# Another written order for tiles 1 to 6 of an attention-plus-MLP kernel, with VectorE's weight sums in other places

## The chip, the cores and the metric

The kernel runs on one core of a Trainium2 chip. The metric is the device time of one execution in microseconds (us), taken as the median of several runs. The core's engines work side by side, each on its own queue in the order in which the program was written: TensorE (PE, matrix products), VectorE (DVE), ScalarE (ACT), GpSimd (POOL) and SyncE (SP, which here only issues DMAs). They wait for each other through semaphores.

## The reference, cut to what matters

```python
# q, k, v: 8 batches x 8 heads x 576 rows x 64
q_s = softmax(q, axis=-1)          # over the 64
k_s = softmax(k, axis=2)           # over the 576 rows
kv  = einsum('bhsd,bhse->bhde', k_s, v)
att = einsum('bhsd,bhde->bhse', q_s, kv)
x   = att.transpose(0, 2, 1, 3).reshape(4608, 512)
h   = x @ w_in                     # 512 x 2048
out = maximum(0.01 * h, h) @ w_out # 2048 x 512
```

Inputs and output are float32 in HBM; the kernel's products are bf16.

## The kernel before, in words

The attention goes batch by batch (b = 0 to 7). The two layers go in nine tiles of 512 tokens (t = 0 to 8). Batch 0, batch 1 and tile 0 are written out call by call and end at about 50.5 us of the profile. Tiles 1 to 6, with the attention of batches 2 to 7 between them, are played from one long list of words, `SCORE` (L799); tiles 7 and 8 from a second list, `WEAVE`. `play` (at the end of the kernel function) takes a word at a time and emits its instructions. A list thus fixes the order on every engine's queue at once; a scheduler does not touch it. Moving a word past words of other engines changes nothing, moving it past words of its own engine does. Rotating buffers are also given out in this order: six PSUM banks for most products (two more for others), six SBUF slots of 9216 bytes per partition for the raw loads and later for sums (`raw`), three output buffers.

The words with a tile number in front (`of_tile`, here for tile t):

- `u<h><p>`: one block of layer 1 on TensorE (`layer1`, L516), four matmuls of 512 columns into one bank (448 in tile 1). `l<h><p>`: the leaky activation that empties it, on ScalarE (`leaky`, L525).
- `P<n><sub><half>`: layer 2 on TensorE (`behind`, L946), four matmuls of 256 columns. Layer 2 is done with seven half-size products instead of eight (a Winograd scheme), so products 5, 6, 7 and 3 take differences of activations: `n0_p` to `n3_p`, subtractions on VectorE (L1003). Product 5 needs n0, product 6 needs n1.
- `q...`: ScalarE copies a partial sum out of PSUM (L1013, L1005). `d...`: VectorE adds the last partial sum and writes an output buffer (L895). `w0`, `w1`: SyncE stores it, four DMAs.
- In tile 6 layer 1 too has seven products: `m<n>_p` (TensorE, L916), `s...` (ScalarE, L980) and `c...` (VectorE, L895).

The words of the attention (`of_batch`, for batch b):

- `lk`, `lq`, `lv`: SyncE issues the load of k, q or v (1152 KB each, L83).
- `kt.0` to `kt.3`: VectorE's tree of maxima over k (L160); `km`: the rest of that maximum (L165 to L185); `ks`, `ksB`: the maximum is subtracted from k (L193), on VectorE for batches 2 to 4 and on GpSimd for 5 to 7; `ke`: exp (ScalarE, L201); `va`, `vb`: v is cast (ScalarE, L211); `kv`: TensorE's k-by-v product (L294); `kr`, `kd`: its normalisation (VectorE L326, ScalarE L332).
- `qm`: row maxima of q (VectorE, L225); `qs`: their subtraction, on GpSimd (L256); `qe`: exp (ScalarE, L264); `qu`: row sums and reciprocals (VectorE, L273, L275); `qn`: normalisation (VectorE, L280, two inputs in SBUF); `qt`: a transposing DMA, issued by SyncE (L457); `A`: TensorE's product that makes the tile's input (L438); `x`: ScalarE copies it out (L429). Batch 2 has q in two parts, `.0` and `.1`.
- `T3` (L666), `F1` to `F4` (`fsums`, L780) and `X6`, `X7`: VectorE's sums over weights and inputs for the seven-product schemes. An `F` subtracts two 128x2048 blocks of w_in in bf16, both in SBUF. Tile 6 is the first user of the F sums.

GpSimd's queue in this part holds ten subtractions: qs2.1, qs2.0, qs3, qs4, ks5, qs5, ks6, qs6, ks7, qs7.

Of the kernel before, what the change touches and what calls it, by code (L numbers as in the profile page):

```python
# [25 lines left out]
def kernel(  # L26
# [772 lines left out]
    SCORE = """  # L799
        1u00 1l00 1u11 1u10 1l10 1l11 1u02 1u04 1u15 kt2.1 kt2.2 kt2.3 1u05 qm2.1 1u12 1l02 qs2.1 qm2.0 1u07  # L800
        1l04 1l15 km2 1u06 qe2.1 1l05 1u13 1l12 qu2.1 qs2.0 qe2.0 1u03 ks2 lk3 1l13 1u01 1l06 1l07 1l01 1u17
        1l17 1l03 1u14 1l14 1u16 1l16 ksB2 1P100 qu2.0 qn2.0 1P101 1P110 1P111 1P200 ke2 1P201 1P210 1n0_0
        1n0_1 qn2.1 1P500 1P501 1P510 1n1_0 lq3 1n1_1 1P211 va2 qt2.0 1q1 1P511 1P600 vb2 1q5 1n3_0 kv2
        1P601 qt2.1 1P300 1n2_0 kr2 1P610 1P611 1n3_1 1P301 1d11 kd2 A2.0 A2.1 A2.2 1P310 1q6 x2.01 x2.00
        1P311 x2.20 T3 lq4 1P700 1n2_1 x2.21 1P701 lv3 1P710 1P711 x2.11 kt3.0 kt3.1 kt3.2 kt3.3 qm3 x2.10
        2u02 2l02 2u12 2l12 2u03 2l03 2u06 2u00 qs3 1d22 1P400 1P401 1P410 va3 vb3 2l00 2l06 qm4 qe3 km3
        1d12 2u14 lk4 1w0 1P411 qs4 2u04 2l04 2u13 2l14 2u01 2l01 2u11 2u07 2l13 qu3 lv4 2u15 2u05 2l11 1q21
        2l05 2l15 2u17 2l17 2l07 ks3 2u10 2l10 2u16 2P100 qn3 2P101 qt3 lk5 2l16 ksB3 ke3 2P200 2n0_0 2n0_1
        2P201 2P210 2P211 2n1_0 2P110 2P111 2q1 2n2_1 2n1_1 2P500 2P501 2d11 2P510 kv3 kr3 2P600 2n3_0 2P511
        2n2_0 kd3 2P601 kt4.0 kt4.1 2P610 2q5 2P611 lk6 A3.0 A3.1 2n3_1 A3.2 2q6 2P300 x3.20 x3.10 x3.01  # L810
        kt4.2 2P700 2P701 2P710 x3.21 1w1 2P711 2P301 2P310 lq5 2P311 x3.11 kt4.3 x3.00 3u02 3l02 2d22 km4
        2P400 ks4 va4 2P401 2P410 2P411 3u00 qe4 ksB4 kt5.0 kt5.1 kt5.2 2q21 lv5 kt5.3 km5 ks5 vb4 3l00 3u06
        3u03 3l03 3u07 qu4 3l06 3u17 3l17 3u01 3l01 2d12 3u11 3l07 3l11 3u10 ke4 3l10 3u04 3l04 3u12 3l12
        3u05 3u14 3l05 kv4 kr4 kd4 3l14 3P100 3u13 3l13 3u15 3u16 3l16 qn4 lq6 3P101 3P110 lv6 3l15 3P200
        2w0 qt4 3P111 3P201 3n0_0 3n0_1 3P210 3P211 3n1_1 3n1_0 3P500 3P501 3P510 3P511 3q1 3P600 3n3_1
        3n3_0 2w1 3P601 kt6.0 va5 vb5 3P610 3q5 ke5 3P611 3d11 3P300 3P301 3P310 A4.0 A4.1 3q6 A4.2 kv5
        3n2_0 3n2_1 x4.00 x4.01 3P311 x4.20 x4.11 kt6.1 3P700 3P701 3P710 3P711 x4.21 x4.10 4u03 lq7 va6
        kt6.2 kt6.3 qm5 4u13 4u02 3d22 qs5 3P400 3P401 3P410 vb6 3P411 4l02 4l13 kr5 kd5 3d12 4l03 4u12 4l12
        4u10 4u00 qe5 4u06 4l06 4l00 4l10 4u16 4u17 4u05 4u01 km6 lk7 qu5 qn5 ks6 4l16 3q21 4u04 4l17 4l04
        4l05 4u07 kt7.0 4l07 4u11 4u15 4l01 4l11 4n0_0 4u14 4l15 4l14 4n0_1 4P100 4P101 4P110 4P500 4P111  # L820
        4q1 4n2_0 4n1_0 lv7 4n1_1 4n2_1 kt7.1 4n3_1 kt7.2 ke6 4P501 4P510 4n3_0 4P511 4P600 kt7.3 4P601
        4P610 4P611 4q6 qt5 A5.0 A5.1 A5.2 4q5 x5.10 kv6 qm6 x5.11 x5.01 3w0 qs6 4P700 4P701 4P710 4P711
        x5.00 x5.21 4P300 4P301 4P310 4d22 km7 x5.20 4P200 4P201 4P210 va7 vb7 kr6 kd6 4P400 4P401 4P211
        4P410 4P411 5u00 5l00 5u02 5l02 5u01 5l01 qe6 4d11 5u06 ks7 4P311 F1 qm7 5u12 qs7 5u07 5l06 5l07
        4q21 qu6 4w1 4d12 5l12 5u03 5l03 5u10 ke7 5u05 5u04 5l04 5u16 qn6 3w1 5l10 5l16 5l05 5u13 5l13 5u15
        5u11 5l11 5u17 5l17 5n0_0 5u14 5n2_0 5l15 5P100 5P101 5P110 5P111 5n2_1 5l14 5n0_1 5P500 5P501 5q1
        5P510 5n1_0 5P600 5n1_1 5P601 5P610 5n3_1 5P611 5q6 qt6 A6.0 x6.00 A6.1 x6.10 A6.2 F2 x6.01 kv7
        x6.20 5P200 x6.21 5P511 x6.11 5P700 5q5 qe7 5P701 5P201 5P210 5P710 5P211 5P711 F3 F4 5n3_0 X6.0 Z0
        X6.1 X6.2 X6.3 kr7 6m5_0 6s5_0 6m5_1 Z1 5d22 6m1_0 5P300 5P301 5P400 6s5_1 kd7 5P401 6m1_2 6m1_1
        6s1_1 5P410 5d11 5P411 6s1_0 5P310 qu7 qn7 qt7 5P311 6m1_3 6s1_2 6m6_2 6m6_0 5q21 Z2 6s6_2 6m2_0 4w0  # L830
        6s6_0 6s1_3 5d12 6c11_0 6l11_0 6m3_0 6c12_0 6m2_1 6m6_1 6c11_1 6m6_3 6s6_1 6m3_1 6m5_3 6c12_1 6s6_3
        6m2_3 6c11_3 6l11_1 6m7_1 6c22_1 6l12_0 6s5_3 6m5_2 6s5_2 6m2_2 6c11_2 6l11_3 6l12_1 6m7_2 6l11_2
        6c22_2 6l22_1 6m3_3 6c12_3 6m3_2 6l12_3 6m7_0 6c22_0 6l22_0 6l22_2 6m7_3 6P100 6c22_3 6P101 5w0
        6m4_1 6m4_0 6l22_3 6P110 6P111 6c12_2 6l12_2 6m4_2 6n0_0 6n1_0 6q1 6l21_1 6m4_3 6l21_0 6P500 6n0_1
        6n1_1 6P600 6P501 6P510 6l21_3 6P601 6P610 6l21_2 6n2_0 6P611 A7.0 A7.1 6q6 A7.2 6P511 x7.20 6P700
        6n2_1 x7.21 6P701 x7.00 6n3_0 6P710 6P711 6q5 6d22 6P200 6P201 5w1 6P210 6P400 x7.11 x7.01 x7.10
        X7.0 X7.1 X7.2 6P401 6P410 6P411 X7.3 6P211 6n3_1 6P300 6q21 6w1 6P301 6P310 6P311 6d11 6d12 6w0
    """.split()
# [304 lines left out]
```

## Time and profile before

| | us |
|---|---|
| median of 3 runs (268.37 to 268.96) | 268.94 |
| the profiled execution | 269.27 |
| its span in the trace | 267.5 |
| busy: TensorE, VectorE, ScalarE, GpSimd | 256.0, 224.7, 192.8, 63.0 |
| granted TensorE clock, mean | 0.995 |

The span is what the trace covers; the remaining 1.77 us of the execution lie around it. "Busy" is the time in which an engine had an instruction running. An engine that waits for a semaphore is idle, but one whose instruction has started and cannot go on counts as busy. The views used are the page, the list of waits, the sums by window, the timeline and the trace's events for DMA landings. A row of the timeline gives start, duration, engine, line of the kernel, operation, output<-inputs, sizes and how many instructions are merged; in brackets stands the idle time just before it and what ended it.

### The profile page before, as it was taken

Reading aid. Unit: us, or ns where it says so; the run is one execution under the profiler, and the core shown is the slowest. Engines: PE = TensorE matmul, PEld = TensorE weight load, DVE = VectorE, ACT = ScalarE, POOL = GpSimd, SP = SyncE. Lnnn points to the kernel's source line nnn. Section 1 sums busy time; section 2 is a strip of 40 time slices with the busy share of each in tenths; the row PEclk is TensorE's granted clock in tenths of the full one; section 3 lists DMA queues with packets and bytes.
Section 4 is the critical chain, followed back from the end, with each engine's and each line's share of the span. In section 5 each row is a group of like instructions: output and inputs, shape, how many; then the busy total and the mean of one; then the engine's idle time right before and its main releaser. Section 6 shows DMA issues by size and latency. Waiting matters only on the chain.

```text
span 267.5 us, 6287 instructions
## 1 busy us (share of the span) xinstructions
PE 256.0 (96%) x2559; PEld 188.9 (71%) x2570; DVE 224.7 (84%) x358; ACT 192.8 (72%) x367; POOL 63.0 (24%) x45
## 2 busy tenths in 40 slices
PE   8689999999999999999999999989999999999992
PEld 3167754457864687458888884478888888888882
DVE  2997899799998998989938989998996589779952
ACT  3977893799769766978797669939697379628920
POOL 2485442250038000250490075600000000000000
PEclk9999999999999999999999999999999999999998
DMA  6999999998983899899952500640194050042004
GB/s 228 349 211 356 316 211 270 340 312 277 258 317 75 234 296 347 283 328 172 340 200 47 122 0 2 157 88 6 22 206 98 22 137 0 2 97 63 0 2 158
DMA packets 37645, 46.48 MB, mean 174 GB/s; under 512 B 18160, under 2 KB 21232, under 8 KB 37616
## 3 DMA queue, kind: packets, MB, share of 16 engines
q1 hardware_dynamic: 32976, 36.64, 47.7%
q0 software_dynamic: 4320, 8.91, 13.3%
q10 hardware_dynamic: 320, 0.52, 0.6%
q8 instruction: 20, 0.33, 0.5%
q14 instruction: 9, 0.07, 0.1%
HBM read 36.70 MB, written 9.44 MB: 172 GB/s over the span
## 4 chain that ended last, share of the span: by engine, by line
PE 78%; DVE 8%; DMA 6%; ACT 2%; issue 1%; POOL 0%; ACTq 0%; POOLq 0%
PE acc L946 36%; PE ph L516 24%; PE ph L916 14%; DMA w_in_sb<-in_moe_w_in_dram 3%; DMA qX<-qe 3%; DVE fs_spare L780 2%; PE po L438 2%; DVE qe L280 1%; DVE qsum L273 1%; DVE qmax L225 1%; DVE gs L1003 1%; PE pkv L294 1%; ACT ke L201 1%; PE po L294 1%; DVE k_raw L380 1%; PE pout L541 1%
## 5 line engine op out<-in xcount | busy, mean ns | idle before, releaser
L516 PE MATMUL ph<-xT,w_in_sb 128*128 128x256 bf16 (+3 forms) x505 | 85.6, 325 | 0.9 <-DMA w_in_sb<-in_moe_w_in_dram 0.2
L516 PEld LDWEIGHTS <-w_in_sb 128*128 128x128 bf16 x512 | 49.8, 98 | 32.8 <-DMA w_in_sb<-in_moe_w_in_dram 0.7
L525 ACT ACTIVATE gj<-ph 128x512 bf16<-128x512 f32 (+2 forms) x116 | 60.4, 580 | 16.3 <-PE ph L516 11.7
L946 PEld LDWEIGHTS <-gs 128*128 128x128 bf16 x512 | 49.4, 98 | 7.7 <-DVE gs L1003 1.1
L256 POOL TENSOR_TENSOR q_raw<-q_raw,qmax 128x2304 f32<-128x2304 f32 (+3 forms) x10 | 29.7, 2975 | 65.5 <-DVE qmax L225 65.5
L946 PEld LDWEIGHTS <-gj 128*128 128x128 bf16 x384 | 37.4, 98 | 5.9
L946 PE MATMUL acc<-w_out_sb,gj 128*128 128x256 bf16 x256 | 32.0, 273 | 0.0
L946 PE MATMUL acc<-wsum,gs 128*128 128x256 bf16 x256 | 30.9, 273 | 0.8 <-DVE gs L1003 0.8
L946 PE MATMUL acc<-w_out_sb,gs 128*128 128x256 bf16 x256 | 31.1, 273 | 0.0
L980 ACT COPY part_spare<-ph 128x512 f32<-128x512 f32 x36 | 19.5, 588 | 12.3 <-PE ph L916 12.0
L895 DVE TENSOR_TENSOR part_spare<-ph,part_spare 128x512 f32<-128x512 f32 x36 | 23.6, 685 | 2.6 <-PE ph L916 1.8
L273 DVE TENSOR_REDUCE qsum<-qe 128x36 f32<-128x2304 bf16 (+4 forms) x11 | 19.7, 1791 | 4.9 <-ACT qe L264 4.7
L895 DVE TENSOR_TENSOR out_sb<-acc,keep 128x512 f32<-128x512 f32 (+1 forms) x26 | 16.5, 639 | 8.5 <-PE acc L946 4.2
L1003 DVE TENSOR_TENSOR gs<-gj 128x1024 bf16<-128x1024 bf16 (+1 forms) x40 | 22.1, 577 | 1.3 <-ACT gj L525 1.3
L280 DVE TENSOR_TENSOR qe<-qe,qrec 128x2304 bf16<-128x2304 bf16 (+4 forms) x12 | 22.4, 1864 | 0.3
L1003 DVE TENSOR_TENSOR gs<-gj,gs 128x1024 bf16<-128x1024 bf16 (+1 forms) x40 | 22.2, 577 | 0.3
L1013 ACT COPY keep<-acc 128x512 f32<-128x512 f32 x22 | 12.8, 589 | 12.5 <-PE acc L946 11.9
L429 ACT CAST xT<-po 128x512 bf16<-128x512 f32 (+3 forms) x47 | 18.6, 494 | 4.2 <-PE po L438 4.0
L193 POOL TENSOR_TENSOR k_raw<-k_raw,kall 128x2304 f32<-128x2304 f32 x3 | 15.2, 5070 | 26.3 <-ACT gj L525 26.3
L916 PEld LDWEIGHTS <-fs_spare 128*128 128x128 bf16 x192 | 18.8, 98 | 2.2
L225 DVE TENSOR_REDUCE qmax<-q_raw 128x36 f32<-128x2304 f32 (+4 forms) x11 | 19.6, 1792 | 0.4 <-DMA q_raw<-in_q_dram 0.4
L916 PE MATMUL ph<-xs_spare,fs_spare 128*128 128x256 bf16 x144 | 19.2, 273 | 0.0
(89 smaller groups left out, 319.3 us busy)
## 6 DMA issues: line engine op xcount, KB each, us to landing
out_dram<-out_sb SPq DMA_DIRECT2D x68, 128.0 KB, 2.4
q_raw<-in_q_dram SPq DMA_DIRECT2D x6, 1152.0 KB, 7.0
v_raw<-in_v_dram SPq DMA_DIRECT2D x6, 1152.0 KB, 6.2
k_raw<-in_k_dram SPq DMA_DIRECT2D x5, 1152.0 KB, 9.0
w_in_sb<-in_moe_w_in_dram POOLq DMA_DIRECT2D x4, 512.0 KB, 7.9
...
```

The lines of the kernel that those rows point to most:

```text
L225: nc.vector.tensor_reduce(out=m, in_=st[b]["q"][:, :, rs], axis=AX.X, op=ALU.max)
L256: eng.tensor_tensor(out=qs, in0=qs, in1=st[b]["qmax", rs.start].unsqueeze(3).to_broadcast([P, HL, n, D]), op=ALU.subtract,)
L273: nc.vector.reduce_sum(out=qsum, in_=st[b]["qe"][:, rs], axis=AX.X)
L280: eng.tensor_tensor(out=qes, in0=qes, in1=st[b]["qrec", rs.start].unsqueeze(3).to_broadcast([P, n, HL, D]), op=ALU.mult,)
L429: eng.copy(out=o, in_=i)
L516: nc.tensor.matmul(ph[:, n0:n1], lhsT=w_in_sb[:, i, j * P : (j + 1) * P], rhs=xT[:, i, (c0 + n0) % NX : (c0 + n0) % NX + n1 - n0], start=( ...
L525: nc.scalar.activation(out=o, in_=ph, func=AF.Prelu, alpha=LEAKY_SLOPE)
L895: nc.vector.tensor_tensor(out=o, in0=x, in1=y, op=ALU.add)
L916: nc.tensor.matmul(bank[x, t, p][:, jj], lhsT=lhs(k, 2 * p + jj), rhs=rhs[:, k], start=(first and k == 0 and jj == 0), stop=(k == 1), skip ...
L946: nc.tensor.matmul(b[:, at_], lhsT=lhs(k)[:, sub * P : (sub + 1) * P], rhs=rhs[:, k], start=(first and k == 0 and at_ == 0), stop=(k % (NK ...
L980: nc.scalar.copy(out=fill(t, kind, p), in_=bank["Z" if kind == "s5" else "X", t, p])
L1003: nc.vector.tensor_tensor(out=o, in0=x, in1=y, op=ALU.subtract)
```

## The change

Only the list `SCORE` is changed: the same words in another order. No instruction is added or removed, and no function is changed. On TensorE and the other engines every instruction up to the start of tile 1 and all of `WEAVE` keep their places. GpSimd's ten subtractions keep their order among themselves. What moves, engine by engine, as far as the prediction speaks of it:

| | before | after |
|---|---|---|
| VectorE around F1 | 4d22 km7 kr6 4d11 **F1** qm7 qu6 4d12 qn6 5n0_0 5n2_0 5n2_1 5n0_1 5n1_0 ... | 4d22 kr6 km7 qm7 4d11 4d12 qu6 qn6 5n0_0 5n1_0 5n3_0 5n2_0 5n0_1 5n1_1 **F1** 5n3_1 5n2_1 F2 F3 F4 |
| VectorE in tile 2 | qu3 ks3 qn3 ksB3 2n0_0 2n0_1 2n1_0 ... | qu3 ks3 ksB3 2n0_0 qn3 2n0_1 2n1_0 2n1_1 ... |
| TensorE, layer 2 of tile 5 | 5P100 to 5P111, then 5P500 5P501 ... | 5P500, then 5P100 to 5P111, 5P501 ... |
| SyncE's loads and stores | lk3 lq3 qt2.0 qt2.1 lq4 lv3 lk4 1w0 lv4 qt3 lk5 lk6 1w1 lq5 lv5 lq6 lv6 2w0 qt4 2w1 lq7 lk7 lv7 qt5 3w0 ... | lq4 lk3 qt2.0 qt2.1 lq3 lv3 lk4 lv5 lq5 lv4 1w0 qt3 lk5 lk6 1w1 qt4 lv6 2w0 2w1 lq6 lq7 lk7 3w1 qt5 lv7 3w0 ... |

The diff, cut to the rows with the places above:

```diff
     SCORE = """
-        1u00 1l00 1u11 1u10 1l10 1l11 1u02 1u04 1u15 kt2.1 kt2.2 kt2.3 1u05 qm2.1 1u12 1l02 qs2.1 qm2.0 1u07
-        1l04 1l15 km2 1u06 qe2.1 1l05 1u13 1l12 qu2.1 qs2.0 qe2.0 1u03 ks2 lk3 1l13 1u01 1l06 1l07 1l01 1u17
...
-        1P311 x2.20 T3 lq4 1P700 1n2_1 x2.21 1P701 lv3 1P710 1P711 x2.11 kt3.0 kt3.1 kt3.2 kt3.3 qm3 x2.10
-        2u02 2l02 2u12 2l12 2u03 2l03 2u06 2u00 qs3 1d22 1P400 1P401 1P410 va3 vb3 2l00 2l06 qm4 qe3 km3
-        1d12 2u14 lk4 1w0 1P411 qs4 2u04 2l04 2u13 2l14 2u01 2l01 2u11 2u07 2l13 qu3 lv4 2u15 2u05 2l11 1q21
-        2l05 2l15 2u17 2l17 2l07 ks3 2u10 2l10 2u16 2P100 qn3 2P101 qt3 lk5 2l16 ksB3 ke3 2P200 2n0_0 2n0_1
...
-        4P610 4P611 4q6 qt5 A5.0 A5.1 A5.2 4q5 x5.10 kv6 qm6 x5.11 x5.01 3w0 qs6 4P700 4P701 4P710 4P711
-        x5.00 x5.21 4P300 4P301 4P310 4d22 km7 x5.20 4P200 4P201 4P210 va7 vb7 kr6 kd6 4P400 4P401 4P211
-        4P410 4P411 5u00 5l00 5u02 5l02 5u01 5l01 qe6 4d11 5u06 ks7 4P311 F1 qm7 5u12 qs7 5u07 5l06 5l07
-        4q21 qu6 4w1 4d12 5l12 5u03 5l03 5u10 ke7 5u05 5u04 5l04 5u16 qn6 3w1 5l10 5l16 5l05 5u13 5l13 5u15
-        5u11 5l11 5u17 5l17 5n0_0 5u14 5n2_0 5l15 5P100 5P101 5P110 5P111 5n2_1 5l14 5n0_1 5P500 5P501 5q1
...
+        1u00 1l00 1u11 1u10 1l10 kt2.1 kt2.2 1u04 1u15 1l04 lq4 1l15 kt2.3 qm2.1 1l11 qs2.1 1u05 qm2.0 1u02
+        1l05 qe2.1 1l02 1u01 1u06 1l01 km2 1u16 qu2.1 1l06 va2 1u07 1l07 qs2.0 1u03 1u14 1u12 qe2.0 1l16
+        1u13 1l12 1u17 1l03 1P100 1P101 1l13 lk3 1P110 ks2 ksB2 qu2.0 1l17 1l14 qn2.0 1n0_0 ke2 1n0_1 1P200
...
+        lv3 kt3.1 x2.01 x2.11 x2.21 1P310 1P311 kt3.2 1P700 1P701 x2.20 1P710 1P711 x2.00 x2.10 2u01 2u00
+        2l00 2u10 2l01 2l10 kt3.3 qm3 qs3 2u02 2u11 va3 2u03 1d22 lk4 2l11 1P400 1P401 1P410 1P411 2u13 2u17
+        vb3 2u12 2l02 lv5 2u06 qe3 2l03 2u16 2l06 qm4 2u04 km3 1d12 2l13 2u07 2l17 2u05 qu3 2l12 2P200 2u14
+        ks3 ksB3 lq5 2l16 2l04 2u15 1q21 2l07 2P100 2l05 2l14 2P101 2P110 2n0_0 qn3 2l15 2n0_1 ke3 2n1_0
+        2n1_1 2n2_1 2n2_0 2P201 2P111 2q1 2P500 2P210 2P211 lv4 kv3 va4 2d11 kr3 2P600 1w0 2P601 2P610 kt4.0
...
+        qt5 A5.0 4n2_1 x5.00 lv7 A5.1 A5.2 kv6 qm6 qs6 4P700 4P701 4P710 4P711 4P300 4P301 4P200 4P201 3w0
+        x5.20 4d22 4P400 4P401 4P410 4P411 x5.21 kr6 km7 kd6 ks7 x5.01 qm7 4P210 4P211 4d11 x5.11 qs7 4P310
+        x5.10 5u06 5l06 5u02 5l02 5u04 5u11 5l04 5u00 qe6 5l00 4P311 va7 4d12 qu6 5u15 5l11 5u05 qn6 5u12
+        4q21 qt6 5l15 5l12 5l05 5u10 5u13 5l13 5u03 5l03 5l10 5u01 5l01 5n0_0 5n1_0 vb7 5u16 5l16 5n3_0 5u07
+        5l07 5u14 5l14 5u17 5l17 5P500 4w1 5n2_0 5P100 5P101 5P110 5n0_1 5n1_1 F1 5P111 5P501 5P510 5P511
+        5n3_1 5q1 5P600 5P601 5P610 5P611 ke7 5q6 A6.0 x6.00 5q5 A6.1 x6.11 A6.2 kv7 x6.20 5n2_1 5P200 x6.21
...
     """.split()
```

More of the change, by code (lines that the diff above doesn't have):

```diff
@@ L799 @@
     SCORE = """
-        1u00 1l00 1u11 1u10 1l10 1l11 1u02 1u04 1u15 kt2.1 kt2.2 kt2.3 1u05 qm2.1 1u12 1l02 qs2.1 qm2.0 1u07
-        1l04 1l15 km2 1u06 qe2.1 1l05 1u13 1l12 qu2.1 qs2.0 qe2.0 1u03 ks2 lk3 1l13 1u01 1l06 1l07 1l01 1u17
-        1l17 1l03 1u14 1l14 1u16 1l16 ksB2 1P100 qu2.0 qn2.0 1P101 1P110 1P111 1P200 ke2 1P201 1P210 1n0_0
-        1n0_1 qn2.1 1P500 1P501 1P510 1n1_0 lq3 1n1_1 1P211 va2 qt2.0 1q1 1P511 1P600 vb2 1q5 1n3_0 kv2
-        1P601 qt2.1 1P300 1n2_0 kr2 1P610 1P611 1n3_1 1P301 1d11 kd2 A2.0 A2.1 A2.2 1P310 1q6 x2.01 x2.00
@@ L805 @@
-        1P311 x2.20 T3 lq4 1P700 1n2_1 x2.21 1P701 lv3 1P710 1P711 x2.11 kt3.0 kt3.1 kt3.2 kt3.3 qm3 x2.10
-        2u02 2l02 2u12 2l12 2u03 2l03 2u06 2u00 qs3 1d22 1P400 1P401 1P410 va3 vb3 2l00 2l06 qm4 qe3 km3
-        1d12 2u14 lk4 1w0 1P411 qs4 2u04 2l04 2u13 2l14 2u01 2l01 2u11 2u07 2l13 qu3 lv4 2u15 2u05 2l11 1q21
-        2l05 2l15 2u17 2l17 2l07 ks3 2u10 2l10 2u16 2P100 qn3 2P101 qt3 lk5 2l16 ksB3 ke3 2P200 2n0_0 2n0_1
-        2P201 2P210 2P211 2n1_0 2P110 2P111 2q1 2n2_1 2n1_1 2P500 2P501 2d11 2P510 kv3 kr3 2P600 2n3_0 2P511
@@ L810 @@
[L810 to L819, printed above, removed]
@@ L820 @@
-        4l05 4u07 kt7.0 4l07 4u11 4u15 4l01 4l11 4n0_0 4u14 4l15 4l14 4n0_1 4P100 4P101 4P110 4P500 4P111
-        4q1 4n2_0 4n1_0 lv7 4n1_1 4n2_1 kt7.1 4n3_1 kt7.2 ke6 4P501 4P510 4n3_0 4P511 4P600 kt7.3 4P601
-        4P610 4P611 4q6 qt5 A5.0 A5.1 A5.2 4q5 x5.10 kv6 qm6 x5.11 x5.01 3w0 qs6 4P700 4P701 4P710 4P711
-        x5.00 x5.21 4P300 4P301 4P310 4d22 km7 x5.20 4P200 4P201 4P210 va7 vb7 kr6 kd6 4P400 4P401 4P211
-        4P410 4P411 5u00 5l00 5u02 5l02 5u01 5l01 qe6 4d11 5u06 ks7 4P311 F1 qm7 5u12 qs7 5u07 5l06 5l07
@@ L825 @@
-        4q21 qu6 4w1 4d12 5l12 5u03 5l03 5u10 ke7 5u05 5u04 5l04 5u16 qn6 3w1 5l10 5l16 5l05 5u13 5l13 5u15
-        5u11 5l11 5u17 5l17 5n0_0 5u14 5n2_0 5l15 5P100 5P101 5P110 5P111 5n2_1 5l14 5n0_1 5P500 5P501 5q1
-        5P510 5n1_0 5P600 5n1_1 5P601 5P610 5n3_1 5P611 5q6 qt6 A6.0 x6.00 A6.1 x6.10 A6.2 F2 x6.01 kv7
-        x6.20 5P200 x6.21 5P511 x6.11 5P700 5q5 qe7 5P701 5P201 5P210 5P710 5P211 5P711 F3 F4 5n3_0 X6.0 Z0
-        X6.1 X6.2 X6.3 kr7 6m5_0 6s5_0 6m5_1 Z1 5d22 6m1_0 5P300 5P301 5P400 6s5_1 kd7 5P401 6m1_2 6m1_1
@@ L830 @@
[L830 to L834, printed above, removed]
@@ L835 @@
-        6n1_1 6P600 6P501 6P510 6l21_3 6P601 6P610 6l21_2 6n2_0 6P611 A7.0 A7.1 6q6 A7.2 6P511 x7.20 6P700
-        6n2_1 x7.21 6P701 x7.00 6n3_0 6P710 6P711 6q5 6d22 6P200 6P201 5w1 6P210 6P400 x7.11 x7.01 x7.10
-        X7.0 X7.1 X7.2 6P401 6P410 6P411 X7.3 6P211 6n3_1 6P300 6q21 6w1 6P301 6P310 6P311 6d11 6d12 6w0
+        1u00 1l00 1u11 1u10 1l10 kt2.1 kt2.2 1u04 1u15 1l04 lq4 1l15 kt2.3 qm2.1 1l11 qs2.1 1u05 qm2.0 1u02
+        1l05 qe2.1 1l02 1u01 1u06 1l01 km2 1u16 qu2.1 1l06 va2 1u07 1l07 qs2.0 1u03 1u14 1u12 qe2.0 1l16
@@ new lines @@
+        1u13 1l12 1u17 1l03 1P100 1P101 1l13 lk3 1P110 ks2 ksB2 qu2.0 1l17 1l14 qn2.0 1n0_0 ke2 1n0_1 1P200
+        1P201 qt2.0 1P210 1P211 1P111 1q1 qn2.1 1n1_0 1P500 1P501 1P510 1P511 1n1_1 1n3_0 1d11 1P600 vb2 kv2
+        1P601 kr2 qt2.1 1q5 lq3 1P300 1P610 1P611 1n3_1 1P301 kd2 1q6 1n2_0 A2.0 A2.1 A2.2 T3 1n2_1 kt3.0
+        lv3 kt3.1 x2.01 x2.11 x2.21 1P310 1P311 kt3.2 1P700 1P701 x2.20 1P710 1P711 x2.00 x2.10 2u01 2u00
+        2l00 2u10 2l01 2l10 kt3.3 qm3 qs3 2u02 2u11 va3 2u03 1d22 lk4 2l11 1P400 1P401 1P410 1P411 2u13 2u17
@@ new lines @@
+        vb3 2u12 2l02 lv5 2u06 qe3 2l03 2u16 2l06 qm4 2u04 km3 1d12 2l13 2u07 2l17 2u05 qu3 2l12 2P200 2u14
+        ks3 ksB3 lq5 2l16 2l04 2u15 1q21 2l07 2P100 2l05 2l14 2P101 2P110 2n0_0 qn3 2l15 2n0_1 ke3 2n1_0
+        2n1_1 2n2_1 2n2_0 2P201 2P111 2q1 2P500 2P210 2P211 lv4 kv3 va4 2d11 kr3 2P600 1w0 2P601 2P610 kt4.0
+        2P611 2q6 2P501 2P510 2P511 kd3 2q5 2n3_0 2P700 2P701 2P710 2P711 kt4.1 qt3 A3.0 x3.01 A3.1 x3.10
+        x3.00 2n3_1 kt4.2 2d22 kt4.3 km4 ks4 A3.2 ksB4 x3.21 qs4 2P300 2P301 2P310 2P311 2P400 2P401 x3.20
@@ new lines @@
+        lk5 x3.11 vb4 2P410 2P411 3u07 3u06 3l06 kt5.0 kt5.1 2q21 3l07 3u00 3l00 3u01 kt5.2 kt5.3 3l01 3u02
+        km5 2d12 3l02 3u16 3l16 3u13 3l13 qe4 3u03 3l03 3u05 lk6 3u11 3l11 3u04 3l04 1w1 3l05 3u12 3u17 3l12
+        ke4 3u10 3l17 3l10 ks5 qu4 3P100 qn4 qt4 3P101 3P110 3P111 3u14 3l14 3n0_0 3u15 3l15 3n0_1 kv4 kr4
+        3n1_0 3q1 3P200 3P201 3P210 3P500 3P501 3P211 3P510 3P511 va5 vb5 3P600 3n1_1 3P601 kd4 3q5 lv6
+        3n3_0 ke5 3n2_0 3P610 3P300 3n3_1 3P611 3P301 3d11 3q6 3P310 kt6.0 A4.0 3n2_1 x4.00 A4.1 2w0 A4.2
@@ new lines @@
+        kt6.1 kt6.2 kt6.3 kv5 3P311 x4.10 x4.20 3P700 3P701 3P710 3P711 x4.11 x4.21 x4.01 4u12 4u02 4u00 qm5
+        4u03 kr5 3d22 kd5 3P400 3P401 2w1 qs5 va6 km6 3P410 3P411 4l02 4l12 4l00 qe5 4u04 3d12 4u16 4u10
+        4l03 4l10 qu5 lq6 4u06 4u17 4l04 qn5 4u15 lq7 4l06 4l16 4l17 lk7 4u01 3q21 ks6 4l01 4n2_0 4u13 4u11
+        4l13 4l15 4u05 4l11 4n0_0 3w1 4l05 4u07 4l07 4u14 kt7.0 4l14 4P100 4P101 4P110 4P111 vb6 4n0_1 4P500
+        4n1_0 4P501 4P510 4q1 4n1_1 ke6 4P511 4q5 4P600 kt7.1 4P601 4P610 4n3_0 4P611 4q6 kt7.2 kt7.3 4n3_1
@@ new lines @@
+        5n3_1 5q1 5P600 5P601 5P610 5P611 ke7 5q6 A6.0 x6.00 5q5 A6.1 x6.11 A6.2 kv7 x6.20 5n2_1 5P200 x6.21
+        x6.10 F2 5P201 5P210 F3 x6.01 F4 qe7 5P211 5d11 5P700 5P300 4w0 kr7 X6.0 Z0 Z1 5P301 5P701 5P710
+        5P711 5P310 X6.1 5P311 X6.2 X6.3 kd7 6m5_0 6s5_0 5d22 6m5_1 6s5_1 5d12 6m1_0 6s1_0 qu7 6m1_3 6m1_1
+        6s1_1 6m2_0 5P400 6c11_0 6m6_0 6s6_0 6s1_3 6m1_2 6s1_2 6m3_0 6l11_0 6c12_0 5P401 5P410 5P411 qn7 Z2
+        6m6_2 5q21 6m5_2 6m6_1 6m2_1 6c11_1 6m3_1 6m2_3 6s6_2 6m6_3 6s6_1 6c12_1 6s5_2 6m3_2 6c11_3 6l12_0
@@ new lines @@
+        6l11_1 6m7_0 6s6_3 6m5_3 6m2_2 6l12_1 6s5_3 6c12_2 6c22_0 6l11_3 6P100 6l22_0 6c11_2 6l11_2 6m7_2
+        6m7_1 6c22_2 6l22_2 6c22_1 6l22_1 6m7_3 6c22_3 6m3_3 6c12_3 6m4_0 6m4_2 6P101 6P110 6P111 6l12_2
+        6m4_3 6n0_0 6P500 6l22_3 6n1_0 6m4_1 6l12_3 6q1 6l21_0 6n0_1 6P600 6P501 6l21_1 6P510 6n1_1 6P601
+        6P610 6P611 qt7 6l21_2 6n3_0 6l21_3 6q6 A7.0 x7.00 6n2_1 A7.1 x7.11 x7.10 6n2_0 A7.2 6P511 6q5 6P700
+        6P701 6P710 6P711 6d22 6P300 x7.01 6P200 6P201 5w0 6P400 6P401 6P410 6P411 x7.20 x7.21 X7.0 6P210
@@ L838 @@
+        5w1 X7.1 6P211 6n3_1 6P301 6q21 6w1 6P310 6P311 6d11 6d12 6w0 X7.2 X7.3
     """.split()
```

## The prediction, as it was put on record

> **What bounds the kernel now.** I read the page's busy row and clock row first, then the sums by window, the list of waits, and last the timelines round the one gap they leave.
>
> ```profile
> PE 256.0 (96%) x2559; PEld 188.9 (71%) x2570; DVE 224.7 (84%) x358; ACT 192.8 (72%) x367; POOL 63.0 (24%) x45
> PEclk9999999999999999999999999999999999999998
> ```
>
> TensorE is busy for 96% of the span at the full granted clock. Where is the rest? The sums by window give the stretch, its length, then the busy time of PE, PEld, DVE, ACT and POOL. The first window begins with the first word of the changed list, the last ends with the last product.
>
> ```profile
> 50.50:160.00 109.50, 109.19 (x1186) 79.37 (x1191) 97.86 (x153) 87.44 (x149) 31.11 (x9) 1.00 0.75 231
> 160.00:180.00 20.00, 19.10 (x117) 10.76 (x121) 19.93 (x15) 13.75 (x21) 8.42 (x2) 1.00 0.39 83
> 180.00:262.60 82.60, 82.59 (x844) 73.39 (x835) 66.08 (x119) 56.23 (x110) 0.00 (x0) 1.00 0.24 55
> ```
>
> In these 212.1 us TensorE idles 0.31 + 0.90 + 0.01 = 1.22 us. The 0.31 are gaps of 0.05 us that the chain of waits puts down to "issue"; at those places matmul records are missing (the next start comes two spacings later), so they are no idle time. A second reading, by the starts: a `u` word takes 0.865 us, a `P` or `m` word 0.437, and nearly every word follows the one before at just that distance. One does not: from 5P500 to 5P501 it is 1.45 us instead of 0.437, **1.01 us** too many. The list of waits names it (total, times, longest), and TensorE's timeline shows it:
>
> ```profile
> PE acc L946 <- DVE gs L1003: 0.8, 1, 0.8
> ```
>
> ```profile
> 175.48 0.60 PE L946 MATMUL acc<-wsum,gs 128*128 128x256 bf16 x4
> 176.93 0.83 PE L946 MATMUL acc<-wsum,gs 128*128 128x256 bf16 x6 [0.85 <-DVE gs L1003]
> ```
>
> So whatever the new order does to VectorE, it can win about 1.0 us and no more, as long as TensorE's words keep their lengths. Why was VectorE late? Its timeline and GpSimd's:
>
> ```profile
> 159.42 6.04 DVE L780 TENSOR_TENSOR fs_spare<-w_in_sb 128x2048 bf16<-128x2048 bf16 x1
> 165.38 2.54 DVE L225 TENSOR_REDUCE qmax<-q_raw 128x36 f32<-128x2304 f32 x1
> 167.84 2.54 DVE L273 TENSOR_REDUCE qsum<-qe 128x36 f32<-128x2304 bf16 x1
> 171.25 3.21 DVE L280 TENSOR_TENSOR qe<-qe,qrec 128x2304 bf16<-128x2304 bf16 x1
> 174.38 2.48 DVE L1003 TENSOR_TENSOR gs<-gj 128x1024 bf16<-128x1024 bf16 x4
> 178.71 1.22 DVE L780 TENSOR_TENSOR fs_spare<-w_in_sb,fs_spare 128x2048 bf16<-128x2048 bf16 x1
> ```
>
> ```profile
> 159.31 5.07 POOL L193 TENSOR_TENSOR k_raw<-k_raw,kall 128x2304 f32<-128x2304 f32 x1
> 168.00 4.05 POOL L256 TENSOR_TENSOR q_raw<-q_raw,qmax 128x2304 f32<-128x2304 f32 x1 [3.62 <-DVE qmax L225]
> ```
>
> The last VectorE row is F2, 1.22 us; F1, of the same size, took 6.04. F1 started 0.11 us after GpSimd's ks7 and ended 1.08 us after it: for 4.82 us it stood still. qn6 (3.21 instead of the 2.54 of qn3) started 0.80 us before the end of qs7, and qn4 (3.10) 0.69 us before the end of ks5. Each has two inputs in SBUF. VectorE instructions with one input (qm, qu, 2.54 us) or with an input in PSUM (`d` words, 0.63 to 0.69) ran beside GpSimd at their usual length. After F1 the queue qm7, qu6, 4d12, qn6, then the subtractions of tile 5, runs without a gap over 0.1 us up to 5n0_1 (176.19 to 176.87), for which 5P501 waits.
>
> **The change, part by part.** I add the rows up in the new order: TensorE's words at the distances above (`kv` 0.76, `A` 0.2 to 0.3) from 50.53 us on; a ScalarE or VectorE word starts when the one before it allows (start to start is its duration less 0.12 on ScalarE and 0.08 on VectorE, as back-to-back rows overlap), or 0.20 us after the end of the TensorE word that it waits for (the distance in released rows). The same sum for the old order gives margins like the trace's (5P200 behind x6.00: 0.00, trace 0.05; 2P700 behind 2q6: 0.27, trace 0.32). It leaves out 0.09 us at each change of product kind, so its times fall behind the trace's by 0.7 us up to 175; margins do not feel that.
>
> *F1.* In the new VectorE order it stands behind 5n0_1. That one needs 5l17, which ends at 173.85 in this sum. GpSimd's last subtraction, qs7, ends at 172.05 in the old trace and earlier now, since qm7 no longer stands behind F1. F1 therefore costs 1.22: VectorE wins 4.82 us ahead of tile 5's subtractions, none of it in itself end time.
>
> *5P501.* TensorE reaches it at 175.24 (5P500, now first, at 173.05; four `P` words and the rest of 5P500 between). 5l17 173.85, then 5n0_1 0.1 + 0.69: 174.65. Margin 0.6, so the 1.01 us go.
>
> *What is late next.* Every hand-over of the new order, in the same way: 5P200 behind x6.00 0.0 (as before), 6P700 behind 6q6 0.27 (as before), kv2 behind vb2 0.35 (before 0.40), 3P201 behind 3l15 0.42, 6P300 behind 6q5 0.46, 4P501 behind 4n0_1 0.6, kv3 behind ke3 0.70. None is negative. I take zero for all; the ends are zero and what the rivals price.
>
> *GpSimd collisions left.* ks5 ends at 115.1, qn4 starts at 115.5; ks6 ends at 139.9 and qn5 starts there; qs7 ends at 167.6 and qn6 starts 0.4 us before. The last lengthens qn6 to about 3.0; 5n0_0 behind it waits for 5l01 (170.5) anyway. Zero; without that cover 0.4 of VectorE's time, against a margin of 1.7 at 5P500.
>
> *SyncE's queue.* lq3 is moved behind lk3, qt2.0 and qt2.1, to the place that lq4 had: issue 67.8, and lq4's data landed 5.9 us later, 73.7. qm3 wants it at 75.1. Cover 1.4 us; before, lq3 landed 9.7 us ahead of use. lv5 and lq5 come forward, into a stretch where they wait for vb2 (68.0) and vb3 (80.7); lv4 waits for qe3 (84.0) and is wanted by va4 at 95.0. 3w1 (2.5 us on SyncE, free at 141.2) now stands ahead of qt5; qt5 is issued at 143.8 and lands 4.6 us later (its row before: 144.4 to 149.0), A5.0 comes at 151.0. lk6 holds up 1w1 and qt4 until vb4 (103.4), long before qn4 (118) releases qt4. All zero.
>
> *VectorE in tile 2.* qn3 goes ahead of 2n0_1 to 2n1_1, ksB3 ahead of qn3. With qm3 at 75.1, qs3 ends at 81.8, qe3 at 84.0, qu3 at 87.0, ksB3 at 89.5, qn3 at 92.5, 2n1_0 at 93.8; 2P600 wants it at 94.8. Margin 1.0; zero.
>
> *X7.2 and X7.3* go behind 6d12 into the idle 0.69 us ahead of 7c11_0, which waits for 7s1_0 there. They fill 0.76. Zero to 0.1.
>
> **Sum.** 269.27 - 1.01 = 268.26 us for the profiled execution, span 266.5. That execution lies 0.33 above the median of the runs shown, so the median comes to **267.9**. About 0.3% (0.8 us) is what a measurement of this kernel can tell from no change; the forecast lies just beyond it.
>
> **Rivals.**
>
> *A new wait eats the gain.* TensorE now arrives 1.0 us earlier at everything behind 5P501. The hand-overs with margins under 0.5 are the candidates, each against a sum good to some 0.1 us; two or three small waits of 0.1 to 0.5 would leave 268.2 to 268.9. Against it: the old order had as many margins of this size, and its trace shows no wait at them. 0.17.
>
> *Slower: lq3 lands late.* The whole path qm3, qs3, qe3, qu3, qn3, 2n1_0 hangs on it, with 1.0 us to spare; beyond that each us costs TensorE one. Loads with nothing ahead of them on the queue landed in 5.3 to 6.6 us, those behind others in 8.1 to 11.9 (lk4, third in its row). lv3, lk4 and now lv5 follow lq3 at once and could draw on the same engines. At lk4's 11.9 it lands at 79.7, 4.6 late: 3.6 us of stall, 271.5. It is slower than before by 0.3% from a landing at 77.9 on. Against it: lq4 had lv3 and lk4 behind it too. 0.16.
>
> *TensorE had room all along.* If its busy rows hid slack, a better order could win more: the weight loads of these windows fill 163.5 of 212.1 us, and even a tenth of the other 48.6 would give 263.1. Against it stand the starts, one column every 0.427 ns with nothing between. 0.02. The Trainium skill's page "Perfetto Trace Analysis", section "Identifying the Most-Contended Engine", speaks for this one: matmul busy time is a bad measure of the distance to the roofline, and the share of weight loads is to be taken (here 71%). In this trace the distance between starts decides, and it leaves no such room.
>
> *It doesn't do what it says.* F1 could meet a subtraction again: excluded above by 5l17 and qs7, unless GpSimd falls some 7 us behind (F1 starts at 175.2, qs7 ends at 167.6). 0.03, at 268.9.
>
> **Chances.** Forecast 0.62 at 267.9, its own range 267.5 to 268.3 (the three runs spread by 0.6). With the room rival, faster by over 0.3% is 0.64; within 0.3% 0.17 + 0.03 = 0.20; slower 0.16. The range runs from 267.4 to 269.2: it takes in the eaten gain and leaves out the late load and the room.
>
> **What the new profile would show.** Right: an F1 row of 1.22 us; no TensorE wait on L1003; window idle sums near 0.3; qm3 at about 75 us, A6.0 1.0 us earlier than 179.7. Wrong: a TensorE wait over 0.2 us anywhere from 50.5 us on; qm3 waiting for the load of q; 5P200 late behind x6.00; a VectorE row lengthened beside GpSimd with a TensorE wait behind it.

## The result, and the profile after

| | before | after |
|---|---|---|
| median of 5 runs, us | 268.94 (268.37 to 269.09) | 267.56 (267.43 to 267.78) |
| the profiled execution, us | 269.27 | 267.72 |
| its span, us | 267.5 | 265.7 |
| ratio of the times, 95% interval | | 0.9954 (0.994 to 0.9969) |

The kernel became 0.46% faster, between 0.31% and 0.6%. Two later measurements of the same kernel, on two other occasions, gave 0.9964 (0.995 to 0.9978) and 0.996 (0.9948 to 0.9972). The gain is thus 0.9 to 1.4 us by the medians; the prediction said 1.0.

The busy row of the page after and, further down the same page, the chain that ended last, followed back from the last instruction:

```profile
PE 256.8 (97%) x2570; PEld 189.1 (71%) x2570; DVE 219.7 (83%) x358; ACT 193.0 (73%) x367; POOL 63.0 (24%) x45
...
PE 85%; DMA 6%; ACT 2%; DVE 1%; issue 0%; POOL 0%; ACTq 0%; POOLq 0%
```

The chain's row on the page before was:

```profile
PE 78%; DVE 8%; DMA 6%; ACT 2%; issue 1%; POOL 0%; ACTq 0%; POOLq 0%
```

VectorE is busy 5.0 us less although it runs the same 358 instructions, and its share of the chain falls from 8% to 1%: the chain no longer leaves TensorE to pass through 5n0_1 and what stood ahead of it. The sums by window, with the same columns as before:

```profile
50.50:160.00 109.50, 109.50 (x1193) 79.34 (x1191) 98.69 (x152) 85.39 (x147) 31.81 (x9) 1.00 0.76 235
160.00:180.00 20.00, 20.00 (x202) 11.85 (x199) 15.21 (x17) 16.61 (x25) 7.69 (x2) 1.00 0.39 83
180.00:262.60 82.60, 81.30 (x765) 72.25 (x752) 65.20 (x119) 55.44 (x109) 0.00 (x0) 1.00 0.23 53
```

The middle window, which held 0.90 us of idle TensorE time, holds none. In the last one TensorE is idle for 1.30 us only because it is done that much sooner. The 0.31 us of "idle" time in the first window of before are gone too, and so are the missing matmul records: this trace holds all 2570. The list of waits of TensorE begins so, and no line of it names L1003:

```profile
PE pout L343 <- POOL zero L105: 1.3, 1, 1.3
PE pkv L294 <- ACT vb L211: 0.8, 1, 0.8
PE kT L354 <- DVE kmax L160: 0.7, 1, 0.7
```

All its entries lie ahead of 50.5 us, in the part that was not changed; for the time from there on the list is empty. VectorE's timeline round F1, GpSimd's, and TensorE's:

```profile
167.76 2.56 DVE L280 TENSOR_TENSOR qe<-qe,qrec 128x2304 bf16<-128x2304 bf16 x1
...
174.29 0.69 DVE L1003 TENSOR_TENSOR gs<-gj 128x1024 bf16<-128x1024 bf16 x1 [0.59 <-ACT gj L525]
175.02 0.69 DVE L1003 TENSOR_TENSOR gs<-gj,gs 128x1024 bf16<-128x1024 bf16 x1
175.63 1.22 DVE L780 TENSOR_TENSOR fs_spare<-w_in_sb 128x2048 bf16<-128x2048 bf16 x1
```

```profile
158.62 5.07 POOL L193 TENSOR_TENSOR k_raw<-k_raw,kall 128x2304 f32<-128x2304 f32 x1
163.64 4.05 POOL L256 TENSOR_TENSOR q_raw<-q_raw,qmax 128x2304 f32<-128x2304 f32 x1
```

```profile
173.46 0.60 PE L946 MATMUL acc<-wsum,gs 128*128 128x256 bf16 x4
173.90 1.91 PE L946 MATMUL acc<-w_out_sb,gj 128*128 128x256 bf16 x16
175.65 2.56 PE L946 MATMUL acc<-wsum,gs 128*128 128x256 bf16 x22
```

F1 takes 1.22 us. 5n0_1 (174.29) no longer waits behind VectorE's own backlog but for ScalarE's 5l17, and ends at 174.98; TensorE reaches 5P501 about 0.6 us later, and the three rows join without a wait. qn6 starts 0.07 us after qs7's recorded end (163.64 + 4.05) and takes its bare 2.56 us.

To compare kernels without the chance of what lies outside, I use **TensorE's stretch**: from the start of 1u00 to the start of the last product. It is 211.79 us before and 210.66 after. The profiled executions differ by 1.55 us, 1.13 of them in the stretch; the rest lies ahead of 50.5 us (0.16) and behind the last product, where nothing was changed. There the time between VectorE's last instruction and the span's end took 3.9 to 4.5 us over the first six profiles; the control run below comes back to it. Of the 1.13 us, 1.01 are the gap at 5P501, and the other 0.11 lie in the six `kv` words, which together take 4.55 us up to the next word's start before and 4.44 after.

### The profile page after: what moved, and what is told of

It is laid out like the page before. It is cut to its first block, busy times and chain, and to the rows that moved or that the text cites. A ratio compares the mean times of both kernels' runs of the same rounds, so it can differ in the third digit from the quotient of the medians.

```text
span 265.7 us, 6286 instructions
## 1 busy us (share of the span) xinstructions
PE 256.8 (97%) x2570; PEld 189.1 (71%) x2570; DVE 219.7 (83%) x358; ACT 193.0 (73%) x367; POOL 63.0 (24%) x45
## 4 chain that ended last, share of the span: by engine, by line
PE 85%; DMA 6%; ACT 2%; DVE 1%; issue 0%; POOL 0%; ACTq 0%; POOLq 0%
PE acc L946 37%; PE ph L516 29%; PE ph L916 14%; DMA w_in_sb<-in_moe_w_in_dram 3%; DMA qX<-qe 3%; PE po L438 2%; PE pkv L294 1%; ACT ke L201 1%; DVE k_raw L380 1%; PE pout L541 1%; PE po L294 1%; ACT vb L211 1%; ACT qe L264 0%; POOL w_in_sb L129 0%; DVE out_sb L895 0%
## 5 line engine op out<-in xcount | busy, mean ns | idle before, releaser
L525 ACT ACTIVATE gj<-ph 128x512 bf16<-128x512 f32 (+2 forms) x116 | 61.1, 578 | 17.8 <-PE ph L516 14.7
L1003 DVE TENSOR_TENSOR gs<-gj 128x1024 bf16<-128x1024 bf16 (+1 forms) x40 | 22.6, 579 | 4.4 <-ACT gj L525 4.4
L1003 DVE TENSOR_TENSOR gs<-gj,gs 128x1024 bf16<-128x1024 bf16 (+1 forms) x40 | 22.3, 579 | 0.5 <-ACT gj L525 0.2
L280 DVE TENSOR_TENSOR qe<-qe,qrec 128x2304 bf16<-128x2304 bf16 (+4 forms) x12 | 21.4, 1784 | 0.3
```

The lines of the kernel that those rows point to most:

```text
L280: eng.tensor_tensor(out=qes, in0=qes, in1=st[b]["qrec", rs.start].unsqueeze(3).to_broadcast([P, n, HL, D]), op=ALU.mult,)
L525: nc.scalar.activation(out=o, in_=ph, func=AF.Prelu, alpha=LEAKY_SLOPE)
L1003: nc.vector.tensor_tensor(out=o, in0=x, in1=y, op=ALU.subtract)
```

## Experiments

"Ratio" is to the kernel before, timed on the same chip in the same session. Theory: F1's stand behind ks7 is the whole loss, and its removal the whole gain. Rivals: the other moves bring something of their own; any collision of a two-input VectorE instruction with GpSimd costs its length, wherever it stands.

**F1 alone.** The kernel before, with one word moved:

```diff
-        4P410 4P411 5u00 5l00 5u02 5l02 5u01 5l01 qe6 4d11 5u06 ks7 4P311 F1 qm7 5u12 qs7 5u07 5l06 5l07
+        4P410 4P411 5u00 5l00 5u02 5l02 5u01 5l01 qe6 4d11 5u06 ks7 4P311 qm7 5u12 qs7 5u07 5l06 5l07
...
-        5P510 5n1_0 5P600 5n1_1 5P601 5P610 5n3_1 5P611 5q6 qt6 A6.0 x6.00 A6.1 x6.10 A6.2 F2 x6.01 kv7
+        5P510 5n1_0 5P600 5n1_1 F1 5P601 5P610 5n3_1 5P611 5q6 qt6 A6.0 x6.00 A6.1 x6.10 A6.2 F2 x6.01 kv7
```

> The order before, with F1 alone moved behind 5n1_1 (its place in the new order). Theory (TensorE's one wait came from F1 standing still behind GpSimd, and the time follows TensorE's waits alone): F1 takes 1.22 us, TensorE has no wait on L1003 near 175 us, 267.5 to 267.9 us, ratio 0.995 to 0.997, as the whole new order. Rival (the new order wins by its other moves, such as 5P500 first or the loads): the ratio stays over 0.998.

Measured: 267.81 us, ratio 0.9951 (0.9939 to 0.9964); TensorE's stretch 210.74. VectorE's row and TensorE's:

```profile
176.41 1.22 DVE L780 TENSOR_TENSOR fs_spare<-w_in_sb 128x2048 bf16<-128x2048 bf16 x1
```

```profile
173.65 1.91 PE L946 MATMUL acc<-w_out_sb,gj 128*128 128x256 bf16 x16
175.40 2.78 PE L946 MATMUL acc<-wsum,gs 128*128 128x256 bf16 x24
```

One word gives what all the moves gave. The same two kernels beside each other on one chip:

> The kernel before with F1 alone moved behind 5n1_1, now on one chip with the kernel after. If F1's move is the whole gain, both give the same ratio to the kernel before within 0.15%, near 0.9955 (TensorE's stretch from 1u00 to its last product about 210.7 us in both). If the other moves are worth something by themselves, the kernel after is faster by 0.3% or more.

> The kernel after, beside the run with F1 alone on one chip: ratio 0.994 to 0.997. The load lq3 landed 6.4 and 8.1 us after its issue in two profiles of this kernel; if that spread is the rule, a third profile lies between 6 and 9 us, and from about 8 us on TensorE loses what goes beyond (0.1 us so far).

Measured: 268.18 us, 0.9962 (0.995 to 0.9974), with F1 alone, and 268.00 us, 0.996 (0.9948 to 0.9972), for the kernel after; stretches 210.73 and 210.66. What the other moves bring by themselves is below what can be measured here. (In the kernel after, lq3 landed 6.0 us after its issue, at the lower edge of the 6 to 9 expected.)

**The unchanged kernel, put through the same treatment.**

> The kernel before, unchanged, as a measure of the noise and of the time behind the last VectorE instruction, which is 4.4 us in the profile before and 3.9 us in the profile after. If that 0.5 us is chance, this run shows values between 3.9 and 4.5, and the ratio lies within 0.999 to 1.001. If it belongs to the new order, it stays at 4.4.

Measured: 269.21 us, ratio 0.9999 (0.999 to 1.0008), stretch 211.75. The gap is there again in TensorE's timeline:

```profile
175.44 0.60 PE L946 MATMUL acc<-wsum,gs 128*128 128x256 bf16 x4
176.89 1.38 PE L946 MATMUL acc<-wsum,gs 128*128 128x256 bf16 x11 [0.85 <-DVE gs L1003]
```

The other question of the expectation came out against chance: the time behind VectorE's last instruction was 4.47 us, as in the kernel before (4.43), while the three profiles of the kernel after have 3.89, 4.03 and 3.97. It thus seems to go with the order. Part of the difference comes back outside the span, where both profiles of the kernel before have 1.78 us and those of the kernel after 2.06 to 2.09. Why is open.

**No ks7.** The kernel before without GpSimd's subtraction of the maximum from k of batch 7:

```diff
-        ... 5u06 ks7 4P311 F1 qm7 ...
+        ... 5u06 4P311 F1 qm7 ...
```

> The order before without ks7: the subtraction of the maximum from k of batch 7 is left out. F1 stays where it was. Theory (GpSimd's subtraction holds F1 up): F1 takes 1.22 us, no TensorE wait near 175 us, ratio 0.995 to 0.997. Rival (F1 is slow at this place for another reason, such as its operands or TensorE's reads of w_in): F1 stays near 6 us and the time at 268.9.

Measured: 268.05 us, ratio 0.9961 (0.9949 to 0.9974), stretch 210.64, no wait on L1003. F1 in its old place:

```profile
159.49 1.22 DVE L780 TENSOR_TENSOR fs_spare<-w_in_sb 128x2048 bf16<-128x2048 bf16 x1
```

So it was not the place as such, but GpSimd's instruction beside it, that made 6.04 of 1.22.

**F1 put back.** The kernel after, with F1 behind 4d11, as in the kernel before (where qm7 follows F1; here it stands ahead of 4d11):

```diff
-        ... 4P210 4P211 4d11 x5.11 qs7 ...
+        ... 4P210 4P211 4d11 F1 x5.11 qs7 ...
...
-        ... 5n0_1 5n1_1 F1 5P111 ...
+        ... 5n0_1 5n1_1 5P111 ...
```

> The new order, with F1 put back behind 4d11, where ks7 runs and qs7 follows at once. Theory: F1 stands still but TensorE does not notice, because 5n0_1 is tied to 5l17 and not to VectorE's queue. If F1 gets its turn between ks7 and qs7 it takes some 4 us (ends near 165) and the ratio stays at 0.995 to 0.996. If GpSimd goes on with qs7 first, F1 takes some 8 us (ends near 169), qn6 ends after 175, TensorE waits 2 to 3 us at 5P500 and the time is 269.8 to 271. Rival (a collision costs what it cost before wherever it falls): 268.6 us, ratio near 0.999, with a TensorE wait of about 1 us.

Measured: 268.06 us, ratio 0.9964 (0.9951 to 0.9977), stretch 210.66. VectorE's rows and GpSimd's:

```profile
161.20 4.08 DVE L780 TENSOR_TENSOR fs_spare<-w_in_sb 128x2048 bf16<-128x2048 bf16 x1
165.21 0.68 DVE L895 TENSOR_TENSOR out_sb<-acc,keep 128x512 f32<-128x512 f32 x1
```

```profile
159.12 5.07 POOL L193 TENSOR_TENSOR k_raw<-k_raw,kall 128x2304 f32<-128x2304 f32 x1
164.16 5.03 POOL L256 TENSOR_TENSOR q_raw<-q_raw,qmax 128x2304 f32<-128x2304 f32 x1
```

F1 collides again, stands 2.86 us, and the time is that of the kernel after. It ends at 165.28 and holds up 4d12 and qu6; qn6 ends at 171.60, in the kernel after at 170.32 (1u00 began 0.51 us later in this execution). 5n0_1 waits for 5l17 all the same, ends at 175.49, and TensorE wants it at 176.05. A collision costs only what hangs behind it. The rival, a price by length, falls.

**F1 one place later.** The kernel before; only VectorE's queue changes:

```diff
-        4P410 4P411 5u00 5l00 5u02 5l02 5u01 5l01 qe6 4d11 5u06 ks7 4P311 F1 qm7 5u12 qs7 5u07 5l06 5l07
+        4P410 4P411 5u00 5l00 5u02 5l02 5u01 5l01 qe6 4d11 5u06 ks7 4P311 qm7 F1 5u12 qs7 5u07 5l06 5l07
```

> The kernel before, with F1 one place later in VectorE's row: behind qm7 instead of ahead of it, so still while GpSimd's ks7 runs. Theory (a stand-still costs only what hangs behind it): qm7 begins at 159.4 and runs its 2.54 us beside ks7, F1 begins at about 161.9, stands until ks7 ends at 164.3 and takes about 3.6 us; qe7 and qs7 are released earlier, TensorE does not wait at 5P501 and the ratio is 0.995 to 0.997. Rival (the stand-still costs in proportion to its length wherever it is): 2.4 of 4.82 us, about half of the 1.0 us gap stays, ratio 0.998.

Measured: 267.91 us, ratio 0.9961 (0.9946 to 0.9976), no wait on L1003:

```profile
159.50 2.54 DVE L225 TENSOR_REDUCE qmax<-q_raw 128x36 f32<-128x2304 f32 x1
161.96 3.58 DVE L780 TENSOR_TENSOR fs_spare<-w_in_sb 128x2048 bf16<-128x2048 bf16 x1
165.47 2.54 DVE L273 TENSOR_REDUCE qsum<-qe 128x36 f32<-128x2304 bf16 x1
```

```profile
159.39 5.07 POOL L193 TENSOR_TENSOR k_raw<-k_raw,kall 128x2304 f32<-128x2304 f32 x1
164.41 5.04 POOL L256 TENSOR_TENSOR q_raw<-q_raw,qmax 128x2304 f32<-128x2304 f32 x1
```

This is the same two instructions exchanged. qm7, which has one input, fills 2.54 us beside ks7; F1 then stands for 2.36 instead of 4.82 us, and qu6, which waits for qe6 (164.96) in any case, starts only 0.5 us later than that. One exchange of neighbours earns the whole gain.

**The margin of lq3.** The rival that ended slower stood on lq3's landing. Three kernels on one chip: the kernel after itself, lq3 second in its row of loads, lq3 third.

```diff
-        1P601 kr2 qt2.1 1q5 lq3 1P300 1P610 1P611 1n3_1 1P301 kd2 1q6 1n2_0 A2.0 A2.1 A2.2 T3 1n2_1 kt3.0
-        lv3 kt3.1 ...
+        1P601 kr2 qt2.1 1q5 1P300 1P610 1P611 1n3_1 1P301 kd2 1q6 1n2_0 A2.0 A2.1 A2.2 T3 1n2_1 kt3.0
+        lv3 lq3 kt3.1 ...
```

(third: `lv3 lk4 lq3 kt3.1`, and no lk4 further down).

> The kernel after itself, on the same chip as the other three, as the yardstick for them: ratio 0.994 to 0.997 to the kernel before by both theories, no wait of TensorE on L1003.

> The kernel after, with lq3 (the load of q of batch 3) moved one place further back on SyncE, behind lv3. After: lq3 issued at 67.8, landed 74.24, qm3 began at 74.94, and the smallest spare time on its path is 1.2 us (2n1_0 ahead of 2P600). If landing follows the place in the row, by the rows of the loads that came second lq3 lands at about 78, qm3 begins some 3.2 us later, TensorE waits about 2.0 us in tile 2 and the ratio to the kernel before is about 1.003 (2 us above the kernel after). If the transfers share the engines in such a way that a second place costs little (landing by 76), TensorE does not wait and the ratio stays at 0.995.

> The kernel after, with lq3 behind lv3 and lk4. By lk4's own row (third, landed 11.9 us after its issue) lq3 lands at about 80 to 81, qm3 begins 5 to 6 us later than after, and if every us beyond the 1.2 us of spare time is one of TensorE's, TensorE waits 4 to 5 us in tile 2: ratio to the kernel before about 1.011 to 1.014. If the words of tile 2 that stand ahead of the wait or a second path absorb part of it, it is less than twice the loss of the run with lq3 in second place.

| | after | second | third |
|---|---|---|---|
| median, us | 268.04 | 270.16 | 275.05 |
| ratio, 95% interval | 0.9964 (0.995 to 0.9978) | 1.0045 (1.003 to 1.006) | 1.0216 (1.0193 to 1.024) |
| lq3 landed (trace's DMA events), us | 76.14 | 77.82 | 81.74 |
| TensorE's stretch, us | 210.89 | 212.87 | 218.34 |

In the second kernel VectorE waits for the load, and TensorE for VectorE:

```profile
77.85 2.55 DVE L225 TENSOR_REDUCE qmax<-q_raw 128x36 f32<-128x2304 f32 x1 [3.05 <-DMA q_raw<-in_q_dram]
80.31 0.68 DVE L895 TENSOR_TENSOR out_sb<-acc,keep 128x512 f32<-128x512 f32 x1
```

```profile
81.05 1.91 PE L946 MATMUL acc<-wsum,gj 128*128 128x256 bf16 x16 [1.43 <-DVE out_sb L895]
```

The size was as expected (2.0 us of stretch), the place was not: the row that TensorE waits for is 1d22, which stands behind qm3 in VectorE's queue and empties the bank that 1P400 wants. That wait is 1.6 us by the starts; the rest comes in pieces of at most 0.2 us at 2u04, in kv3, round 2P600 and in kv4.

With lq3 third, the same wait has 4.89 us (5.06 by the starts), but the stretch is 7.7 us longer than in the first profile of the kernel after (7.5 than in the one beside it, which had lost 0.2 itself). TensorE's rows, and then the sums of 4 us each (the granted clock is the third figure from the right):

```profile
84.96 3.57 PE L946 MATMUL acc<-wsum,gj 128*128 128x256 bf16 x16 [4.89 <-DVE out_sb L895]
```

```profile
76.00:80.00 4.00, 4.00 (x19) 1.76 (x18) 0.00 (x0) 3.35 (x6) 0.00 (x0) 1.00 1.06 398
80.00:84.00 4.00, 0.07 (x1) 0.00 (x0) 2.24 (x1) 1.38 (x2) 0.00 (x0) 0.94 1.00 337
84.00:88.00 4.00, 3.04 (x15) 2.11 (x15) 3.96 (x5) 0.00 (x0) 3.56 (x1) 0.50 0.46 179
88.00:92.00 4.00, 3.95 (x15) 1.69 (x15) 3.30 (x9) 2.61 (x2) 4.00 (x2) 0.71 0.14 13
92.00:96.00 4.00, 4.00 (x19) 1.79 (x19) 3.97 (x4) 3.01 (x7) 0.50 (x1) 1.00 0.87 271
```

The sixteen products that took 1.91 us take 3.57. The clock record stands at one half from 83.53 to 90.35 us, so the 5.4 us of work up to there did half of what they could. By the starts 2.6 us were lost in them, which with the 5.06 make up the 7.7. My expectation (1.011 to 1.014) priced the wait and not what follows from it.

**lq3 early.** The kernel after, with lq3 back behind lk3 (`1l13 lk3 lq3 1P110`); measured twice.

> The kernel after with lq3 back in its old place on SyncE, right behind lk3 and ahead of qt2.0 and qt2.1. Theory: it lands several us before qm3 wants it, qm3 begins at 74.9 to 75.2 in every execution, TensorE loses nothing there; the gain against the kernel after is 0 to 0.2 us, so the ratio is 0.994 to 0.997. Rival: lq3 ahead of them holds up the transposing transfers qt2.0 and qt2.1 (A2.0 later than 71.1), and TensorE waits there: ratio above 0.997.

> The kernel with lq3 in its old place once more. Its times fell into two groups, seven at 267.7 to 268.3 us and five at 269.0 to 269.7, and its profile was of the first group. If the second group is the late landing of qt2.0 and qt2.1 (spare time 0.9 us in the first profile, landing at 70.65 ahead of A2.0 at 71.57), a profile of an execution above 269 shows TensorE waiting 0.8 to 1.3 us at A2.0 for the DMA into qX. If it is something else, that wait is missing in it. A profile at 268 again tells nothing on this.

Measured: 268.25 us, ratio 0.998 (0.9965 to 0.9995), and 268.09 us, 0.9975 (0.9962 to 0.9988). Both profiles (267.98 and 268.07 us) show what the theory wanted: lq3 lands at 68.7, qm3 starts at 75.3 and 75.2, A2.0 is not late, the stretch is 210.7 and 210.8. But both ratios lie above 0.997, on the rival's side, because the times fall into two groups: 16 of the 24 at 267.4 to 268.4, eight at 269.0 to 269.7, where no run of the kernel after lies. No profile of the second group was taken. In the two that I have, qt2.0 and qt2.1 land at 69.7 and 70.6 instead of 67.6 and 69.5, 0.9 us ahead of A2.0. That they come later still in the second group, so that TensorE waits at A2.0, is a guess and not shown.

## Why the prediction was right

- **What bounds the kernel, and the cap of 1.0 us.** It held, but for 0.11 us in the `kv` words that the sum did not have. TensorE's stretch fell by 1.13 us against the gap of 1.01, and its rows now join. The first measurement's 1.38 us is more than the stretch gives; beside the two others (0.88 and 1.15 us by the medians) it is partly chance. The rival that TensorE "had room all along" falls: with weight loads still busy for 71% of the span, the new order won the gap and hardly more, and the starts now leave no gap from 50.5 us on but the 0.1 us or so at each change of product kind.
- **The cause: F1 beside ks7.** Shown three ways: without ks7, with F1 elsewhere, and with F1 one place later. Here two statements of the Trainium skill's page "SBUF — State Buffer" agree with the trace. Its section "Who interferes with whom" says that a VectorE instruction with two inputs in SBUF contends with a GpSimd instruction that reads SBUF. Its section "Terms" says that the port pair which the two engines share is held for the full instruction while the other blocks. The trace shows it in both directions: F1 stood 4.82, 2.86 and 2.36 us until ks7 had ended, and qs7 took 5.03 and 5.04 us instead of 4.05 where F1 had got in ahead of it.
- **5P501's margin.** Reckoned 0.6, measured 0.56 (5n0_1 ends at 174.98, the first weight load of 5P501 starts at 175.54).
- **The other hand-overs.** None became a wait in the first profile. 5P200 follows x6.00 by 0.05 (reckoned 0.0). Two margins that the list did not name are as small, 7P700's and 8P700's with 0.09.
- **GpSimd collisions left.** qn6 was to meet qs7 by 0.4 us and grow to 3.0. It started 0.07 us behind it and took 2.56. qn4, reckoned to start 0.4 us behind ks5, started 0.38 ahead of its end and took 2.79. Such a reckoning is thus good to some 0.5 to 0.8 us here; neither cost anything.
- **lq3.** The forecast of 73.7 was close (74.24 in the first profile, 73.71 in a third), but 76.14 in the second, 8.2 us after the issue: qm3 waited 1.07 us for it, which the prediction had named as a sign of being wrong, and TensorE lost about 0.13 us at 2P601. The three landings lie 2.4 us apart, which is more than the cover of 1.4, so the cover alone does not make the term zero; most of the lateness went into the 1.2 us to spare behind qm3. That it did not cost more was in part luck. The rival was to be slower by 0.3% from a landing at 77.9 on; with a landing at 77.82 it was slower by 0.45% (0.3 to 0.6), so the point was about right.
- **Where a step failed.** "The whole path qm3, qs3, qe3, qu3, qn3, 2n1_0 hangs on it ... beyond that each us costs TensorE one." There is a second path, qm3, 1d22, 1P400, with 1.5 us to spare where the named one has 1.2; it comes first, so most of the wait appeared on it. And one for one is true only of short waits: at 4.9 us the clock took another 2.7. The price of 271.5, for 3.6 us of stall, stood at the edge of that.
- **SyncE's other moves, tile 2, X7.2 and X7.3.** Zero each, as reckoned; 2P600's margin was 1.2 (reckoned 1.0). qt3 needed 6.5 us to land and left 0.8 us ahead of A3.0, a thin place that the prediction did not list.
- **One sign misread.** A6.0 was to come 1.0 us earlier than 179.7. It came at 178.80, 0.85 earlier, although the gap is gone: in the new order 5P511 (0.44 us) stands ahead of it as well, which the prediction left out.
